# Moving query loads, masks and list products in an attention, dense and routed MLP kernel

## The chip, the cores and the metric

The kernel runs on one core of one Trainium2 chip. The metric is the device time of one execution in microseconds; the figure for a kernel is the median of its runs. A profile is taken of a separate execution, which has its own time and its own span (from the first to the last instruction).

## The reference

A delta-rule attention over 4 batches x 8 heads, 768 positions, 48 channels; then a dense gated MLP on the 3072 resulting tokens; then a routed MLP in which each token goes to one of 8 experts. Cut to what is computed:

```python
# attention, per batch and head
k_n = k / (norm(k) + 1e-6)
for t in range(768):
    y[t] = q[t] @ state
    v_old = k_n[t] @ state
    state += beta[t] * outer(k_n[t], v[t] - v_old)
# dense MLP ("MoE 1"), x is 3072 x 384
x = ((x @ w1) * (x @ w2)) @ w3 @ w_out
# routed MLP ("MoE 2")
logits = x @ w_gate + modality_bias[modality_id]
e_idx = argmax(logits); gate_w = softmax(logits)[e_idx]
out[mask_e] = gate_w * (relu(x[mask_e] @ w1[e]) @ w2[e])      # for each expert e
```

## The kernel before

**Stages.** `startup` (0 to about 120 us) decodes the dense weights, which arrive as raw 64-bit words, and folds `w3 @ w_out` into one matrix (product `pw`, 64 matmuls in 8 groups, the last operands of which, `wos`, lie partly in the buffer `X[1]`, called X_91 in the trace). Then `moe1(i)` runs 12 times, once for each tile of 256 tokens (about 41 us each). Each has 8 sub-steps `f`; a sub-step multiplies one slice of the first two weight matrices (`pAB`, 18 matmuls), evicts it (`a`, `ch`, `cl`), and two sub-steps later multiplies it by the folded matrix (`px`). At last `moe2` runs 14 slots of at most 256 tokens of one expert; a slot has 8 sub-steps of 9 matmuls `ph` and, two later, 6 matmuls `spy` (or `px` in every other slot).

**Attention steps.** The attention is cut into 12 steps `s` of 64 positions. Step `s` is done inside the tile `moe1(s - 1)`, by `slot(s, f)`. Its chain on TensorE: `chain_k` at f = 0 (keys times the state X, product `pk` or `pkq`), `chain_u` at f = 2 or 3 (`pu`), `chain_y` at f = 4 (`py`, the output), `chain_s` at f = 6 (`pS`, the next state). Every step also needs keys times queries with a causal mask, written over the queries, which lie beside the state in the same buffer (columns D and up of `X`, called W). From step 2 on state and queries are multiplied jointly: one matmul of 112 columns for the 48 of the state and the 64 of the queries (`pkq`). Steps 0 and 1 multiply the queries on their own (`masked`, product `pq`).

**PSUM rings.** Two pools of two buffers each, `ps` and `pc`. The joint product takes four buffers: quarters 0 and 1 from `ps`, 2 and 3 from `pc`. VectorE first subtracts the state's part of all four (R), then masks quarters 0 and 1 at f = 0; `mask_parts` yields, and quarters 2 and 3 are masked at f = 1. `chain_u`, `chain_y` and `chain_s` take buffers of `pc`; the products of `merge1`, `merge2`, `gram` and `place` take buffers of `ps`.

**Order.** Every engine's instructions are issued in the order in which the program is written (class `Engine` chains them), the DMA queue of SyncE (SP) too: an instruction that waits holds back all that stand behind it on its engine.

**Routed part.** `place` finds for each tile of tokens the place in the expert's list: a position (`pr`, then `pos`, `hi`, `lo` on VectorE), one-hot factors (`hot`), and their product `pl`, which is added to `list`. For the last tile this is done inside slot 0 of `moe2` by the generator `late`, of which `back` takes one piece in each sub-step; it goes on with the list (`listed`), and the table of the remaining slots (`late_slots`, `tif`), from which the token gathers of slot 3 and later start. `tokens2` transposes the gathered tokens of the next slot (`spt`, one product in each of three sub-steps) and splits them (`sxh` on ScalarE, `sxl` on VectorE); `weights` splits the next slot's weights (`w1h`, `w1l`, `w2h`, `w2l`). Two lines set their order in a sub-step:

```python
ahead(f in (1, 2, 3), 1 + (f < 3 if i == 0 else f > 4))   # back: tokens in which f, how many weight pieces
for _ in range(n): next(work, None)                        # step: weight pieces first, then tokens
```

Of the kernel before, what the change touches and what calls it, by code (L numbers as in the profile page):

```python
# [8 lines left out]
F32 = mybir.dt.float32  # L9
# [7 lines left out]
ALU = mybir.AluOpType  # L17
# [4 lines left out]
P = 128  # L22
B, H, S, D = 4, 8, 768, 48
NT, DM, DFF, E = 3072, 384, 1024, 8
NPAIR = H // 2
C = 64
# [79 lines left out]
class Kernel:  # L106
# [60 lines left out]
    def slot(self, s, f):  # L167

        if s >= NS:
            return  # L170
        u, c = divmod(s, US)
        self.at(s + f / FC)
        more = u + 1 < NUNIT
        if f == 0:
            self.chain_k(s)
            if s == 1:
                self.queries(1)
                self.queries(2)
        elif f == 1:
            if c == 0:  # L180
                list(self.merge1(u))
                next(self.work, None)
                if more:
                    self.work = self.inverse(u + 1)
            if s > 1:
                list(self.masks)
        elif f == 2:
            list(self.chain_u(s) if c else self.merge2(u))
            if s == 1:
                list(self.masked(s))  # L190
            if s + 1 < NS:
                self.values(s + 1)
        elif f == 3:
            if c == 0:
                list(self.chain_u(s))
            if c == 1 and u + 2 < NUNIT:
                self.keys(u + 2)
        elif f == 4:
            list(self.chain_y(s))
        elif f == 5:  # L200
            if s + 2 < NS:
                self.queries(s + 2)
            if c == 1 and u + 2 < NUNIT:
                self.prep(u + 2, range(0, NP, HP))
        elif f == 6:
            if s + 1 < NS:
                list(self.chain_s(s))
        elif f == 7:
            if s + 2 < NS:
                self.tokens(s + 2)  # L210
            if c == 1 and u + 2 < NUNIT:
                self.prep(u + 2, range(NP, NU, HP))
# [204 lines left out]
    def masked(self, s):  # L417

        nc, ps = self.nc, self.ps
        kT, W, n0 = self.st[s // US]["kT"], self.st["W", s], s % US * NP  # L420
        mb = self.mask.unsqueeze(1).to_broadcast([P, HP, C])
        todo = []
        for a in range(0, NP, HP):
            pq = ps.tile([P, HP, C], F32, tag="ps", name="pq")
            for n in range(HP):
                for h in range(2):
                    o, w = (1 - h) * C, h * C
                    nc.tensor.matmul(pq[o:o + C, n], kT[w:w + C, n0 + a + n], W[w:w + C, h, a + n], start=True, stop=True)
            todo.append((a, pq))
        yield  # L430
        for a, pq in todo:
            for h in range(2):
                o = (1 - h) * C
                if s < 1:
                    nc.scalar.copy(W[o:o + C, h, a:a + HP], pq[o:o + C])
                    nc.gpsimd.affine_select(out=W[o:o + C, h, a:a + HP], in_=W[o:o + C, h, a:a + HP], pattern=[[0, HP], [1, C]], compare_op=ALU.is_gt, fill=0.0, base=0, channel_multiplier=-1)
                    continue
                nc.vector.tensor_tensor(out=W[o:o + C, h, a:a + HP], in0=pq[o:o + C], in1=mb[o:o + C], op=ALU.mult)

    halves = range(0, NP, HP)  # L440

# [3 lines left out]
    def chain_k(self, s):  # L445

        nc, a1, pc = self.nc, self.a1, self.pc
        kT, n0, vt = self.st[s // US]["kT"], s % US * NP, self.st["v", s]
        self.scaled(s)
        if s == 0:  # L450
            self.R = vt
            return
        X = self.X[self.xi]
        R = a1.tile([P, NP, D], F32, tag="R", name="R")
        if s > 1:
            todo = []
            for q, a in enumerate(range(0, NP, NQ)):
                pool, tag = ((self.ps, "ps"), (pc, "pc"))[q // 2]
                pk = pool.tile([P, NQ, D + C], F32, tag=tag, name="pkq")
                for m in range(NQ):  # L460
                    for h in range(2):
                        o, w = (1 - h) * C, h * C
                        nc.tensor.matmul(pk[o:o + C, m], kT[w:w + C, n0 + a + m], X[w:w + C, h, a + m], start=True, stop=True)
                todo.append((a, pk))
            for a, pk in todo:
                nc.vector.tensor_tensor(out=R[:, a:a + NQ], in0=vt[:, a:a + NQ], in1=pk[:, :, 0:D], op=ALU.subtract)
            self.R = R
            self.masks = self.mask_parts(s, todo)
            next(self.masks)
            return  # L470
        for a in self.halves:
            pk = pc.tile([P, HP, D], F32, tag="pc", name="pk")
            for n, m, h in self.tiles(a):
                o, w = (1 - h) * C, h * C
                nc.tensor.matmul(pk[o:o + C, m], kT[w:w + C, n0 + n], X[w:w + C, h, n, 0:D], start=True, stop=True)
            nc.vector.tensor_tensor(out=R[:, a:a + HP], in0=vt[:, a:a + HP], in1=pk, op=ALU.subtract)
        self.R = R

    def mask_parts(self, s, todo):

        W = self.st["W", s]
        mb = self.mask.unsqueeze(1).to_broadcast([P, NQ, C])
        for q, (a, pk) in enumerate(todo):
            for h in range(2):
                o = (1 - h) * C
                self.nc.vector.tensor_tensor(out=W[o:o + C, h, a:a + NQ], in0=pk[o:o + C, :, D:], in1=mb[o:o + C], op=ALU.mult)
            if q == 1:
                yield
# [72 lines left out]
    def startup(self):  # L561
# [173 lines left out]
            do.setdefault(FC + 8 + x, []).append(lambda: next(rs, None))  # L735
        do.setdefault(t + 4, []).append(lambda: self.parts_x(0))
        folded = todo.index(("3", K3 - 1))
        do.setdefault(folded, []).append(self.clear)
        do.setdefault(folded + 1, []).append(lambda: split(self.chain_s(0)))
        do.setdefault(NSTART - 1, []).extend([lambda: self.tokens(1), lambda: self.tokens(2)])  # L740
        for n in range(-1, NSTART):
# [339 lines left out]
    def moe2(self, early, cur):  # L1081
# [3 lines left out]

        def late():
            yield
            yield from self.place(NT // MT - 1)
            yield
            yield from self.listed()  # L1090
            yield
            yield from self.late_slots()
# [22 lines left out]
        def ahead(i):  # L1115

            self.upto = i + 2
            toks = iter(self.tokens2(todo[i + 1], states[i + 1])) if i + 1 < len(kinds) else iter(())

            def step(tok, n):  # L1120
                for _ in range(n):
                    next(work, None)
                if tok:
                    next(toks, None)

            return step, toks
# [129 lines left out]
    def back(self, i, mi, ahead):  # L1256
# [11 lines left out]
        for f in range(FC):  # L1268
# [9 lines left out]
            hl = s3.tile([P, SLOT], F32R, tag="hl", name="hl", bufs=SLAG + 2)  # L1278
            nc.scalar.activation(hh, ph, AF.Relu)
            nc.vector.scalar_tensor_tensor(out=hl, in0=ph, scalar=0.0, in1=hh.bitcast(F32), op0=ALU.max, op1=ALU.subtract)  # L1280
            ahead(f in (1, 2, 3), 1 + (f < 3 if i == 0 else f > 4))
            if i < NEARLY:
                next(self.late, None)
            elif i > NEARLY + 1:
# [105 lines left out]
```

## Time and profile before

| | us |
|---|---|
| median of 3 runs | 841.74 (840.85 to 842.69) |
| the profiled execution, its own time | 841.03 |
| its span | 839.3 |
| TensorE busy in the span | 786.3 |
| VectorE busy | 618.8 |
| ScalarE busy | 408.9 |
| GpSimd busy | 165.6 |

The profiled execution's time is 1.7 us longer than its span, and 0.7 us below the median of the runs. Busy time is summed over instructions that overlap in part, so it tells which engine leads, not how much work is left. Each row of the timeline gives the start, the duration, the engine, and the tile written and the tiles read; in square brackets stands how long the engine sat idle before it and what ended that.

### The profile page before, as it was taken

The page shows a single profiled execution, that of the slowest core. Times are in us where ns is not written, and L with a number is a line of the kernel's source. Part 1 is how long each engine was busy: PE and PEld are TensorE (multiplying, and loading weights), DVE is VectorE, ACT ScalarE, POOL GpSimd, SP SyncE. Part 2 cuts the span into 40 slices and gives each one's busy share as a digit, 9 for nine tenths or more (in the row PEclk, how much of TensorE's full clock was granted, in tenths as well). Part 3 has the DMA queues.
Part 4 walks back from the last instruction along what each step waited for, and adds up shares of the span by engine and source line. Part 5 has one row for each costly group of instructions (what it writes and reads, how often), then busy time and mean ns, then how long its engine had stood idle before and what let it go on. Part 6 is the DMA issues. An engine that isn't in the chain of part 4 may idle for free.

```text
span 839.3 us, 23624 instructions
## 1 busy us (share of the span) xinstructions
PE 786.3 (94%) x9583; PEld 730.6 (87%) x9583; DVE 618.8 (74%) x1573; ACT 408.9 (49%) x863; POOL 165.6 (20%) x172
## 2 busy tenths in 40 slices
PE   5797789999999999999999999999899999999994
PEld 5664468999999899989998999999799999999983
DVE  5998889769777976897689864567886778677651
ACT  6467673562546154524543353334455655655541
POOL 3021121100000001000100000013254654645420
PEclk8598899999999999999999999999999999999997
DMA  9952563314121421133021401047457678677610
GB/s 310 280 176 87 151 161 102 75 35 120 54 51 38 116 65 40 40 115 82 23 65 39 102 13 31 27 131 222 151 177 246 215 249 258 227 225 238 220 56 6
DMA packets 71812, 105.34 MB, mean 126 GB/s; under 512 B 33988, under 2 KB 53332, under 8 KB 71696
## 3 DMA queue, kind: packets, MB, share of 16 engines
q1 hardware_dynamic: 64464, 88.35, 34.7%
q0 software_dynamic: 4064, 11.06, 3.9%
q10 hardware_dynamic: 3168, 4.34, 1.5%
q8 instruction: 77, 1.26, 0.6%
q14 instruction: 39, 0.32, 0.1%
HBM read 89.15 MB, written 10.63 MB: 119 GB/s over the span
## 4 chain that ended last, share of the span: by engine, by line
PE 46%; DVE 26%; issue 11%; ACT 7%; POOL 4%; DMA 3%; SPq 1%; POOLq 0%; DVEq 0%; ACTq 0%
PE pAB L86 13%; PE px L86 9%; PE ph L86 7%; PE spy L86 4%; DVE tmp L86 4%; DVE Tt L86 4%; DVE X L86 3%; DVE TT L86 2%; PE pw L86 2%; DVE Ab L86 2%; ACT TT L86 2%; PE pkq L86 2%; PE pg L86 2%; DVE a L86 2%; PE py L86 2%
## 5 line engine op out<-in xcount | busy, mean ns | idle before, releaser
L86 PE MATMUL pAB<-x,w 128*128 128x256 f32 x1728 | 228.8, 286 | 0.0
L86 PEld LDWEIGHTS pAB<-x,w 128*128 128x128 f32 x1728 | 213.9, 191 | 4.4
L86 ACT CAST ch<-a 128x256 fp32r<-128x256 f32 x96 | 39.0, 406 | 116.4 <-DVE a L86 116.4
L86 ACT COPY a<-pAB 128x256 f32<-128x256 f32 x96 | 35.6, 371 | 116.9 <-PE pAB L86 104.3
L86 DVE TENSOR_TENSOR a<-a,pAB 128x256 f32<-128x256 f32 x96 | 40.0, 416 | 65.6 <-ACT a L86 65.3
L86 PE MATMUL ph<-sxh,w1h 128*128 128x256 f32 x288 | 82.5, 286 | 0.5 <-DVE hl L86 0.5
L86 ACT ACTIVATE hh<-ph 128x256 fp32r<-128x256 f32 x96 | 37.0, 385 | 91.7 <-PE ph L86 91.5
L86 PE MATMUL ph<-sxl,w1h 128*128 128x256 f32 x288 | 81.2, 282 | 0.0
L86 PE MATMUL ph<-sxh,w1l 128*128 128x256 f32 x288 | 81.2, 282 | 0.0
L86 DVE SCALAR_TENSOR_TENSOR hl<-ph,hh 128x256 fp32r<-128x256 f32 x96 | 40.3, 420 | 41.0 <-ACT hh L86 40.5
L86 DVE TENSOR_TENSOR Tt<-tmp,Tt 128x31 f32<-128x31 f32 (+15 forms) x186 | 64.3, 346 | 6.4
L86 DVE TENSOR_TENSOR w2l<-r,w2h 128x768 fp32r<-128x768 f32 x56 | 59.5, 1074 | 12.2 <-ACT w2h L86 11.9
L86 DVE TENSOR_TENSOR tmp<-Ab,Tt 128x31 f32<-128x31 f32 (+15 forms) x186 | 65.4, 352 | 3.0
L86 PE MATMUL px<-w34h,ch 128*128 128x392 f32 x192 | 65.6, 342 | 0.0
L86 PE MATMUL px<-w34h,cl 128*128 128x392 f32 x192 | 65.3, 340 | 0.0
L86 PE MATMUL px<-w34l,ch 128*128 128x392 f32 x192 | 65.2, 339 | 0.0
L86 POOL TENSOR_TENSOR w1l<-r,w1h 128x512 fp32r<-128x512 f32 x39 | 51.0, 1327 | 49.9 <-ACT w1h L86 49.6
L86 DVE TENSOR_TENSOR cl<-a,ch 128x256 fp32r<-128x256 f32 x96 | 43.0, 447 | 20.1 <-ACT ch L86 19.3
L86 PEld LDWEIGHTS ph<-sxh,w1h 128*128 128x128 f32 x288 | 54.7, 190 | 1.3 <-DVE hl L86 1.1
L86 PEld LDWEIGHTS ph<-sxh,w1l 128*128 128x128 f32 x288 | 54.8, 190 | 0.0
L86 PEld LDWEIGHTS ph<-sxl,w1h 128*128 128x128 f32 x288 | 54.6, 190 | 0.0
L86 ACT CAST w1h<-r 128x512 fp32r<-128x512 f32 x84 | 49.5, 615 | 2.9 <-DMA r<-in_e_w_dram 2.5
(269 smaller groups left out, 1677.7 us busy)
## 6 DMA issues: line engine op xcount, KB each, us to landing
r<-in_e_w_dram SPq DMA_DIRECT2D x42, 512.0 KB, 4.7
r<-in_e_w_dram SPq DMA_DIRECT2D x56, 384.0 KB, 3.9
raw<-in_w_dram SPq DMA_DIRECT2D x28, 512.0 KB, 4.6
kT<-in_kt_dram SPq DMA_DIRECT2D x12, 512.0 KB, 4.5
X<-in_q_dram SPq DMA_DIRECT2D x24, 256.0 KB, 4.8
vt<-in_v_dram SPq DMA_DIRECT2D x12, 384.0 KB, 4.7
kb<-in_kb_dram SPq DMA_DIRECT2D x12, 384.0 KB, 4.7
x2d<-xr ACTq DMA_DIRECT2D x22, 192.5 KB, 2.8
```

The source lines that it names most:

```text
L86: x = f(*a, **kw)
```

## The change

It does five things.

1. Step 1 multiplies state and queries jointly as well (`chain_k`); its mask is applied by a ScalarE copy and a GpSimd select (`mask_parts`) in place of VectorE's products, in eight pieces of 64 x 256. `masked` is left with step 0 alone.
2. The query loads of steps 1 and 2 are issued in `startup`, when the last fold has been issued, in place of sub-step 0 of tile 0.
3. The joint product's rings change places with the step's parity: odd steps take quarters 0 and 1 from `pc`, 2 and 3 from `ps`.
4. In slot 0 of the routed part the product `pl` and its addition to `list` come one sub-step later; in slot 0 the next slot's token piece comes ahead of the weight pieces of the sub-step.
5. In slot 2 the transposes for slot 3 come in sub-steps 3, 4, 5 in place of 1, 2, 3.

```diff
@@ slot @@
         if f == 0:
             self.chain_k(s)
-            if s == 1:
-                self.queries(1)
-                self.queries(2)
...
-            if s > 1:
-                list(self.masks)
+            list(self.masks)
         elif f == 2:
             list(self.chain_u(s) if c else self.merge2(u))
-            if s == 1:
-                list(self.masked(s))
@@ chain_k @@
+        for q, a in enumerate(range(0, NP, NQ)):
+            pool, tag = ((self.ps, "ps"), (pc, "pc"))[(q // 2 + s) % 2]
-                pool, tag = ((self.ps, "ps"), (pc, "pc"))[q // 2]
...
-        for a in self.halves:
-            pk = pc.tile([P, HP, D], F32, tag="pc", name="pk")
...
@@ mask_parts @@
+                if s == 1:
+                    self.nc.scalar.copy(W[o:o + C, h, a:a + NQ], pk[o:o + C, :, D:])
+                    self.nc.gpsimd.affine_select(out=W[o:o + C, h, a:a + NQ], in_=W[o:o + C, h, a:a + NQ], pattern=[[0, NQ], [1, C]], compare_op=ALU.is_gt, fill=0.0, base=0, channel_multiplier=-1)
+                    continue
@@ startup @@
-        do.setdefault(folded, []).append(self.clear)
+        do.setdefault(folded, []).extend([self.clear, lambda: self.queries(1), lambda: self.queries(2)])
@@ moe2, late @@
-            yield from self.place(NT // MT - 1)
+            last = self.place(NT // MT - 1)
+            next(last)
             yield
+            next(last)
+            yield
+            yield
+            list(last)
             yield from self.listed()
@@ moe2, step @@
+                if tok and i == 0:
+                    next(toks, None)
                 for _ in range(n):
                     next(work, None)
-                if tok:
+                if tok and i > 0:
                     next(toks, None)
@@ back @@
-            ahead(f in (1, 2, 3), 1 + (f < 3 if i == 0 else f > 4))
+            ahead(f - 2 * (i == 2) in (1, 2, 3), 1 + (f < 3 if i == 0 else f > 4))
```

The DMA queue of SP at the end of `startup`; `raw` are pieces of the dense weights, X_91 and X_90 the buffers of the queries of steps 1 and 2, `kb` the keys by token of steps 1 and 2. Before:

```order
L86 DMA raw<-in_w_dram 128x512 x13
L86 DMA kb<-in_kb_dram 128x768 x2
L86 DMA X_91<-in_q_dram 64x16x64 x2
L86 DMA X_90<-in_q_dram 64x16x64 x2
L86 DMA vt<-in_v_dram 128x768
```

and now:

```order
L86 DMA raw<-in_w_dram 128x512 x12
L86 DMA X_91<-in_q_dram 64x16x64 x2
L86 DMA X_90<-in_q_dram 64x16x64 x2
L86 DMA raw<-in_w_dram 128x512
L86 DMA kb<-in_kb_dram 128x768 x2
```

The four query loads went ahead of the last weight piece and of the two `kb` loads.

TensorE at sub-step 3 of slot 0 of the routed part, where the list's product `pl` reads `hot`; the `spy` behind it is of sub-step 1. Before:

```order
L86 MATMUL ph<-sxh,w1l 128x256
L86 MATMUL spt<-ident,xg 128x128 x2
L86 LDWEIGHTS hot
L86 MATMUL pl<-hot 128x192
L86 LDWEIGHTS hot
L86 MATMUL pl<-hot 128x192
L86 MATMUL spy<-w2h,hh 128x384
```

and now, with the `ph` of sub-step 4 ahead of it and the `spy` of sub-step 2 behind:

```order
L86 MATMUL ph<-sxh,w1l 128x256
L86 LDWEIGHTS hot
L86 MATMUL pl<-hot 128x192
L86 LDWEIGHTS hot
L86 MATMUL pl<-hot 128x192
L86 MATMUL spy<-w2h,hh 128x384
```

The list's product stands 15 matmuls later (6 `spy` and 9 `ph`).

VectorE at sub-step 1 of the same slot, where `sxl` frees the buffer that the second transpose waits for, and `pos` begins the last tile's placing. Before:

```order
L86 SCALAR_TENSOR_TENSOR hl<-ph,hh 128x256
L86 TENSOR_TENSOR w1l<-r,w1h 128x512
L86 TENSOR_TENSOR sxl<-spt,sxh 128x256
L86 TENSOR_TENSOR pos<-pr,cnt 128x16
L86 TENSOR_TENSOR cnt<-pr,cnt 128x8
```

and now:

```order
L86 SCALAR_TENSOR_TENSOR hl<-ph,hh 128x256
L86 TENSOR_TENSOR sxl<-spt,sxh 128x256
L86 TENSOR_TENSOR w1l<-r,w1h 128x512
L86 TENSOR_TENSOR pos<-pr,cnt 128x16
L86 TENSOR_TENSOR cnt<-pr,cnt 128x8
```

The token split and one weight piece changed places.

## Rows read from the trace of the kernel before

**Rows 1.** The page: busy us of each engine, share of the span, instructions.
```profile
PE 786.3 (94%) x9583; PEld 730.6 (87%) x9583; DVE 618.8 (74%) x1573; ACT 408.9 (49%) x863; POOL 165.6 (20%) x172
```

**Rows 2.** TensorE's waits over the whole span: us in total, times, longest us.
```profile
PE pu L86 <- DVE X L86: 4.1, 4, 1.4
...
PE py L86 <- DVE X L86: 1.6, 3, 1.0
...
PE pkq L86 <- DVE list L86: 1.0, 2, 0.6
```

**Rows 3.** Timeline, TensorE, step 5 (start us, us, engine, instruction, idle before).
```profile
283.03 2.52 PE L86 MATMUL pkq<-X,kT 64*64 64x112 f32 x48 [0.61 <-DVE list L86]
...
293.09 2.07 PE L86 MATMUL pu<-R,TT 64*64 64x48 f32 x64 [0.87 <-DVE X L86]
```

**Rows 4.** Timeline, VectorE, step 5: the two mask parts of the joint product.
```profile
288.10 1.73 DVE L86 TENSOR_TENSOR X<-pkq,mask 64x256 f32<-64x256 f32 x4
...
292.09 1.75 DVE L86 TENSOR_TENSOR X<-pkq,mask 64x256 f32<-64x256 f32 x4
```

**Rows 5.** Timeline, TensorE: step 1's two products, and step 3's joint one.
```profile
118.81 2.12 PE L86 MATMUL pk<-X,kT 64*64 64x48 f32 x64 [0.41 <-ACT X L86]
...
127.31 1.97 PE L86 MATMUL pq<-X,kT 64*64 64x64 f32 x60
...
200.02 3.37 PE L86 MATMUL pkq<-X,kT 64*64 64x112 f32 x64
```

**Rows 6.** Timeline, VectorE: step 1's masks.
```profile
136.06 2.85 DVE L86 TENSOR_TENSOR X<-pq,mask 64x512 f32<-64x512 f32 x4
```

**Rows 7.** Timeline, GpSimd and SP: what waits for the last fold, the last weight piece.
```profile
114.98 2.80 POOL L86 MEMSET X<- 32x1536 f32 x2 [19.40 <-PE pw L86]
...
116.38 0.33 SPq L86 DMA_DIRECT2D raw<-in_w_dram  x1
```

**Rows 8.** Landing of query loads: the four of steps 1 and 2.
```profile
DMA to landing us min/median/max: 5.7/7.7/8.0
```

**Rows 9.** The same for one later step's pair, and SP's issue of it.
```profile
190.45 1.30 SPq L86 DMA_DIRECT2D X<-in_q_dram  x2
...
DMA to landing us min/median/max: 4.0/4.3/4.6
```

**Rows 10.** Timeline, GpSimd and VectorE: step 0's selects, VectorE under them and alone.
```profile
53.88 3.33 POOL L86 TENSOR_SCALAR_AFFINE_SELECT X<-X 64x512 f32<-64x512 f32 x4 [45.24 <-ACT X L86]
...
53.98 0.67 DVE L86 TENSOR_TENSOR tmp<-Ab,Tt 128x112 f32<-128x112 f32 x1
...
82.40 0.27 DVE L86 TENSOR_TENSOR tmp<-Ab,Tt 128x112 f32<-128x112 f32 x1
```

**Rows 11.** Stretches: length, then PE, PEld, DVE, ACT, POOL busy (count), PEclk, DMA.
```profile
95.70:102.50 6.80, 3.41 (x5) 1.85 (x6) 6.56 (x13) 3.87 (x9) 0.00 (x0) 0.50 0.49 163
...
597.50:600.80 3.30, 3.30 (x15) 3.30 (x14) 1.39 (x3) 0.00 (x0) 0.00 (x0) 0.50 0.52 204
```

**Rows 12.** Timeline, TensorE, slot 0: the waits, and the spy of sub-step 2.
```profile
592.13 0.44 PE L86 MATMUL spt<-ident,xg 128*128 128x128 f32 x2 [1.15 <-DVE sxl L86]
...
596.75 0.64 PE L86 MATMUL pl<-hot 128*128 128x192 f16 x2 [1.84 <-DVE hot L86]
...
600.90 0.34 PE L86 MATMUL spy<-w2h,hh 128*128 128x384 f32 x1
```

**Rows 13.** Timeline, VectorE, slot 0: token split, and the hl of sub-steps 2 and 3.
```profile
591.66 0.42 DVE L86 TENSOR_TENSOR sxl<-spt,sxh 128x256 fp32r<-128x256 f32 x1
...
595.54 0.42 DVE L86 SCALAR_TENSOR_TENSOR hl<-ph,hh 128x256 fp32r<-128x256 f32 x1
...
597.00 0.42 DVE L86 SCALAR_TENSOR_TENSOR hl<-ph,hh 128x256 fp32r<-128x256 f32 x1
```

**Rows 14.** Timeline, TensorE, slot 2: its first product, and the wait for gathered tokens.
```profile
628.04 0.28 PE L86 MATMUL ph<-sxh,w1h 128*128 128x256 f32 x1
...
632.04 0.33 PE L86 MATMUL spt<-ident,xg 128*128 128x128 f32 x1 [1.59 <-DMA xg<-x2d,id]
```

More of the change, by code (lines that the diff above doesn't have):

```diff
@@ L420, in masked @@
         kT, W, n0 = self.st[s // US]["kT"], self.st["W", s], s % US * NP
-        mb = self.mask.unsqueeze(1).to_broadcast([P, HP, C])
         todo = []
@@ L433, in masked @@
                 o = (1 - h) * C
[L434 to L438, printed above, removed]
+                nc.scalar.copy(W[o:o + C, h, a:a + HP], pq[o:o + C])
+                nc.gpsimd.affine_select(out=W[o:o + C, h, a:a + HP], in_=W[o:o + C, h, a:a + HP], pattern=[[0, HP], [1, C]], compare_op=ALU.is_gt, fill=0.0, base=0, channel_multiplier=-1)
     halves = range(0, NP, HP)
@@ L454, in chain_k @@
         R = a1.tile([P, NP, D], F32, tag="R", name="R")
-        if s > 1:
-            todo = []
-            for q, a in enumerate(range(0, NP, NQ)):
-                pool, tag = ((self.ps, "ps"), (pc, "pc"))[q // 2]
[L459 to L470, printed above, removed]
-        for a in self.halves:
-            pk = pc.tile([P, HP, D], F32, tag="pc", name="pk")
[L473 to L476, printed above, removed]
+        todo = []
+        for q, a in enumerate(range(0, NP, NQ)):
+            pool, tag = ((self.ps, "ps"), (pc, "pc"))[(q // 2 + s) % 2]
+            pk = pool.tile([P, NQ, D + C], F32, tag=tag, name="pkq")
+            for m in range(NQ):
+                for h in range(2):
+                    o, w = (1 - h) * C, h * C
+                    nc.tensor.matmul(pk[o:o + C, m], kT[w:w + C, n0 + a + m], X[w:w + C, h, a + m], start=True, stop=True)
+            todo.append((a, pk))
+        for a, pk in todo:
+            nc.vector.tensor_tensor(out=R[:, a:a + NQ], in0=vt[:, a:a + NQ], in1=pk[:, :, 0:D], op=ALU.subtract)
         self.R = R
+        self.masks = self.mask_parts(s, todo)
+        next(self.masks)
     def mask_parts(self, s, todo):
```

## The prediction

> **What bounds the kernel now.** I read the page first: TensorE is busy in 94% of the span, the next engine, VectorE, in 74% [rows 1]. So the time is TensorE's own work plus its waits, and an edit is worth what it takes from either. The table of TensorE's waits then shows which waits the change can touch [rows 2], and the timeline of one place each shows what the wait hangs on: in the odd attention steps [rows 3, 4], in step 1 [rows 5 to 9], in slot 0 of the routed part [rows 12, 13], and in slot 2 [rows 14]. The reader is to see in the rows that these waits are short (0.4 to 1.8 us) and that each ends with a VectorE instruction or a transfer that stands late in its order, not with one that lacks time. Last comes the granted clock by stretches: there are stretches in which TensorE ran at 1.2 GHz, the lower level, and one of them follows on the waits of slot 0 [rows 11].
>
> **Rings by parity (odd steps).** In step 5 `pu` waits 0.87 us for a mask [rows 3]: `chain_u` takes its two buffers from `pc`, and there quarters 2 and 3 of the joint product lie, which are masked last, from 292.09 on; quarters 0 and 1 are done at 288.10 + 1.73 = 289.83 [rows 4]. Now quarters 0 and 1 lie in `pc`. `pu` would be reached at 293.09 - 0.87 - 0.61 = 291.6 (the 0.61 is the wait of the next sentence), 1.8 us after its buffers are free. That 1.8 us is the cover: if VectorE ran later by more than that, the rest would come back as a wait. There are four such waits, 4.1 us in all [rows 2]. The joint product itself waits in two odd steps for the `list` addition, which frees a `ps` buffer, 1.0 us in all [rows 2, 3]; it now begins in `pc`, and comes to `ps` half a product (1.7 us of the 3.37 in rows 5) later, over the longest of these waits, 0.6. Nothing is late next: the second mask part is then needed only by `py`, two sub-steps on, and the even steps keep their rings. Sum: -5.1, bounds 0 and -5.1; I take -5.1, because the rows name the masks and the list as what ended these waits.
>
> **Step 1, joint.** Removed: the state's product, 2.12, and the queries' own, 64/60 of 1.97 = 2.10; added: a joint one, 3.37 in step 3 [rows 5]. That is -0.85 on TensorE. VectorE loses four masks, 2.85 us [rows 6], behind which `py` waited three times, 1.6 us in all [rows 2]; that wait goes, since the masks now go to ScalarE and GpSimd sub-steps before `py`. Together -2.45.
>
> Against it stands that the joint product needs the queries at once. Their loads write into X_91, where the last fold still reads. The GpSimd clearing of the same buffer begins at 114.98, released by that fold [rows 7], and the loads can't be issued before it either. A pair takes 1.30 us to issue [rows 9], so the second goes out at about 115.65. To its landing the rows give two prices: 4.0 to 4.6 us for a pair with nothing ahead of it [rows 9], and 5.7 to 8.0 for these very loads, which before had a weight piece and two `kb` loads ahead of them [rows 7, 8]. The bounds are thus 115.65 + 4.0 = 119.7 and 115.65 + 8.0 = 123.6. I take 4.6, so 120.3, because of the three loads ahead only one weight piece is left, issued earlier. TensorE was to begin at 118.81 [rows 5], so it waits 1.5 us longer. Sum of step 1: -2.45 + 1.5 = -0.9. The bounds: -2.45 if no wait is added, +2.4 at 123.6.
>
> A rule bears on that choice. The Trainium skill, DMA: Bandwidth & Descriptors, section Queues, rings and completion order, says that a DMA engine takes up descriptors of one queue in the order of its ring. By it the two loads for step 2 and the weight piece behind them can't hold up those of step 1, and the sum would be the -0.9; with the longest landing seen here it would be +2.4. The rows of before do not separate the two, since there the heavier loads were ahead as well as beside.
>
> The eight GpSimd selects are half the size of step 0's, four of which took 3.33 us [rows 10]: 8 x 0.42 = 3.3 us on an engine that is busy for a fifth of the span. VectorE isn't free of them: a product over 112 columns took 0.67 us under those selects and 0.27 without [rows 10]. Four products so stretched by 0.4 us are 1.6 us, less than the 2.85 us of masks that VectorE loses. The Trainium skill, SBUF — State Buffer, section Who interferes with whom, has a harder rule: a VectorE instruction with two inputs in SBUF and a GpSimd one that reads SBUF block each other for the whole instruction. By it VectorE could lose all 3.3 us, 0.5 more than it gains, and the wait of `py` would come back with about 0.5 us of its 1.6; the trace shows the stretching, and does not show whether it is whole.
>
> ScalarE gets eight copies of 64 x 256. VectorE's masks of that shape take 1.73 / 4 = 0.43 [rows 4]; at that price it is 3.5 us on an engine that is busy for half of the span, spread over two sub-steps, and I cost it at nothing. If that cover were gone, `a` of the same sub-step would be late by it, and `pAB` two sub-steps on behind that. On SP the four loads now stand ahead of the last weight piece (116.38 before, rows 7) and of two `kb` loads. Four at 0.65 us each from 115.0 put the piece at 117.6 or later; it is decoded in tile 0 and `kb` is first needed at sub-step 6, so I cost this at nothing too, and return to it below.
>
> **Slot 0 of the routed part.** The second transpose waited 1.15 us for `sxl`, which ended at 592.08; it now stands ahead of one weight split, whose place began 0.6 us earlier [rows 12, 13]: -0.6. The list's product waited 1.84 us up to 596.75, so TensorE was there at 594.91 [rows 12], now at 594.3. It goes on with six `spy` (0.175 us each, 1.05), to 595.35. The `ph` of sub-step 4 then needs the buffer that `hl` of sub-step 2 frees at 595.54 + 0.42 = 595.96 [rows 13]: a new wait of 0.6. Nine `ph` at 0.117 take it to 597.05, where `hot` is ready (`hl` begins behind it at 597.00, rows 13); the product takes 0.2, and the `spy` of sub-step 2 begins at 597.3 in place of 600.90 [rows 12]: -3.6. Of that 1.65 is the low clock: the stretch from 597.50 to 600.80 ran at 1.2 GHz [rows 11], half speed for 3.3 us. I take it that the clock stays up, because the waits of this place (1.15 and 1.84 among them) shrink to about 1.2 us. If it falls all the same, the sum is -1.95. The addition to `list` comes a sub-step later than before, but `listed` still follows in the same sub-step as before, so the chain to the table is not lengthened.
>
> **Slot 2.** The transposes waited 1.59 us for gathered tokens, to 632.04 [rows 14]. Slot 2 would begin at 628.04 - 3.6 = 624.4. The new place is four `ph` groups and one `spy` group in, 5.3 us, so 629.7. The table on which the gathers hang is made by VectorE in pieces behind the `hl` of each sub-step, so it moves up with TensorE by some part of 3.6: tokens between 628.4 and 632.0, a wait between 0 and 2.3. I take 0, as the pieces follow TensorE's sub-steps: -1.6; the other end is +0.7.
>
> **Sum.** -5.1 - 0.9 - 3.6 - 1.6 = -11.2. The profiled execution took 841.03, so 829.8; the median of the runs was 0.7 above it (841.74), so 830.5.
>
> **Rivals.**
> - *The stall of step 1 pulls the clock down.* TensorE is idle for about 1.9 us before the joint product (from 118.4, its wait of before included), more than either wait in slot 0 that was followed by 1.2 GHz. For it: the stretch from 95.7 to 102.5, in which TensorE was busy for only half, ran at 1.2 GHz throughout [rows 11]. Against it: the wait of 1.59 in slot 2 stands alone and is no longer than that by much, and no fall of the clock is among its rows. One such stretch costs 1.65: 832.2. With the late landing (+3.3) and 6.8 us at half speed (3.4): 837.2.
> - *The gain of the routed part is eaten.* The clock falls in slot 0 anyway (+1.65), and the tokens of slot 3 do not move up (+2.3): 834.4. For it: VectorE is the engine that ends every wait there. Against it: the two long waits shrink by more than half.
> - *The rings don't do it.* The `pu` waits stay because VectorE is late in general, and only the list waits go: +4.1, so 834.6. Against it: the first masks are done 1.8 us before `pu` is reached.
> - *Slower.* The query loads, four with 64-column pieces, and the weight piece behind them hold TensorE up at step 1. Each microsecond of landing past 120.3 costs one, and the low clock 3.4 more. That eats the whole gain at 120.3 + 11.2 - 3.4 = 128.1, 12.5 us after issue; at 16 us after issue (131.6) the kernel would take 841.7 + 3.5 = 845.2. The longest landing in the rows is 8.0 [rows 8], so this needs a queue twice as slow as any seen.
>
> **How the numbers follow.** Chances: the forecast 0.44, the stall with the clock 0.29, the routed part 0.11, the rings 0.06, slower 0.05, and 0.05 for several losses together that end near the time before. Likeliest: 830.5. The range goes from 828.8 (no wait for the queries, -1.5 more) to 837.2, and leaves out the last two cases and the tails. A measurement of this kernel tells some 0.2% (1.7 us) from no change; so faster 0.90, same 0.05, slower 0.05.
>
> **What would show it.** Right: no waits of `pu` for masks and of `pkq` for `list` in steps 3 to 9; the joint product of step 1 at about 120.3; no wait of `py` in step 1; full clock in slot 0 and the `spy` of its sub-step 2 about 3.6 us earlier against the slot's start; no wait for `xg` in slot 2. Wrong: a joint product of step 1 after 122 or with PEclk 0.5 behind it, new waits of `pAB` for `a` in tile 0 or for `hl` in slots 0 and 1, or tokens of slot 3 that come no earlier than before.

## Result and the profile after

The changed kernel takes 832.33 us (median of 4 runs, 829.90 to 832.64), the kernel before 842.22 (4 runs). The ratio is 0.9878, with a 95% interval of 0.9855 to 0.9901: faster by 1.2%, some 10 us. The forecast was 830.5 in a range of 828.8 to 837.2, so the time lies 1.8 us above the forecast and inside the range. Measured again for the experiments (e5 below), the same kernel took 832.03 against 840.36, a ratio of 0.9895 (0.9877 to 0.9914).

The profiled execution took 832.64 us, with a span of 830.4. From the page, as in [rows 1]:

```profile
PE 782.0 (94%) x9519; PEld 727.6 (88%) x9519; DVE 617.9 (74%) x1571; ACT 410.9 (49%) x871; POOL 170.0 (20%) x180
```

TensorE is busy 4.3 us less and the span is 8.9 us shorter; the rest, about half, is time in which TensorE waited. The table of TensorE's waits (us in total, times, longest), to be read against [rows 2]; rows of the startup, which differ by up to 1.2 us either way, are left out, as are waits that stayed as they were:

```profile
PE ph L86 <- DVE hl L86: 1.5, 2, 1.1
...
PE pkq L86 <- ACT X L86: 1.4, 1, 1.4
...
PE pkq L86 <- DMA X<-in_q_dram: 1.0, 1, 1.0
PE pkq L86 <- ACT An L86: 0.7, 2, 0.4
...
PE spt L86 <- DVE sxl L86: 0.5, 1, 0.5
...
PE spy L86 <- DVE hl L86: 0.2, 1, 0.2
```

The waits of `pu` and `py` for masks, of `pkq` for `list`, of `pl` and of `spt` for `xg` are gone. New are the two waits of step 1's joint product (1.4 and 1.0), a longer one for `hl` in slot 0, and one of `spy`; the wait of `pkq` for `An` grew from 0.2 to 0.7.

To see where the time went, the span is cut at six starts that can be read from TensorE's timeline: the first `pS`, the `pAB` of sub-step 4 of tile 0, and the first `ph` of slots 0 to 3. Each column is a difference of two such starts (us), for every kernel profiled here:

| kernel | to first pS | step 1 | rest of MoE 1 | slot 0 | slot 1 | slot 2 | slot 3 to end |
|---|---|---|---|---|---|---|---|
| before | 116.76 | 23.28 | 446.58 | 23.71 | 17.71 | 19.43 | 191.83 |
| after | 116.26 | 24.44 | 440.72 | 20.60 | 17.71 | 18.56 | 192.11 |
| e1 rings off | 117.07 | 27.14 | 446.40 | 20.60 | 17.71 | 18.94 | 191.84 |
| e2 rings only | 116.94 | 23.24 | 440.84 | 22.16 | 17.71 | 19.17 | 191.84 |
| e3 step 1 old | 117.34 | 23.25 | 440.78 | 20.63 | 17.71 | 18.92 | 193.07 |
| e4 fill | 116.20 | 21.21 | 440.84 | 20.60 | 17.74 | 19.20 | 191.71 |
| e5 after again | 116.54 | 22.41 | 440.76 | 20.62 | 17.71 | 19.81 | 192.65 |
| e6 before again | 116.26 | 23.26 | 446.16 | 23.71 | 17.72 | 19.52 | 191.77 |
| e7 pl back | 117.76 | 22.55 | 440.93 | 24.04 | 17.74 | 18.72 | 191.76 |
| e8 tokens back | 116.27 | 22.56 | 440.96 | 20.21 | 17.72 | 19.24 | 191.74 |
| e9 slot 2 back | 117.66 | 22.35 | 440.86 | 20.62 | 17.72 | 19.49 | 191.90 |
| e10 fewer pieces | 116.88 | 22.32 | 440.77 | 20.61 | 17.73 | 17.77 | 196.02 |
| e11 three edits | 115.57 | 21.24 | 441.07 | 20.23 | 17.71 | 17.74 | 197.84 |
| e12 step 2 later | 115.58 | 22.41 | 440.70 | 20.61 | 17.74 | 18.44 | 191.92 |

Where nothing was edited, "rest of MoE 1" and slots 0 and 1 repeat within 0.4 us. The other columns do not: without an edit in them the startup differs by up to 2.2 us between executions, slot 2 and the last column by 1.4 each. So effects below 2 us are read from the columns and not from the total times, and in slot 2 not from one profile.

Step 1 in the changed kernel, on TensorE (start, us, engine, instruction, idle before and what ended it), and PEclk behind it in the view by stretches (columns as in [rows 11]):

```profile
116.26 1.64 PE L86 MATMUL pS<-X,kb 64*48 64x48 f32 x64
119.33 0.37 PE L86 MATMUL pkq<-X,kT 64*64 64x112 f32 x2 [1.43 <-ACT X L86]
120.69 4.91 PE L86 MATMUL pkq<-X,kT 64*64 64x112 f32 x62 [0.98 <-DMA X<-in_q_dram]
...
130.04 2.07 PE L86 MATMUL pu<-R,TT 64*64 64x48 f32 x64
...
138.68 2.08 PE L86 MATMUL py<-X 128*64 128x64 f32 x64
...
122.00:125.40 3.40, 3.40 (x40) 3.32 (x35) 1.87 (x5) 2.44 (x6) 1.38 (x4) 0.50 1.00 328
```

The joint product stalls twice, for 2.41 us together, and then 62 of its matmuls take 4.91 us, because the clock fell to 1.2 GHz. `pu` and `py` wait for nothing any more.

Slot 0, TensorE, as in [rows 12]: the second transpose, the `ph` of sub-step 4, the list's product:

```profile
586.32 0.44 PE L86 MATMUL spt<-ident,xg 128*128 128x128 f32 x2 [0.54 <-DVE sxl L86]
...
591.21 0.39 PE L86 MATMUL ph<-sxh,w1h 128*128 128x256 f32 x1 [1.07 <-DVE hl L86]
...
592.37 0.34 PE L86 MATMUL pl<-hot 128*128 128x192 f16 x2
```

`pl` no longer waits, `spt` waits 0.61 less than before, and the wait for `hl` that the forecast put at 0.6 is 1.07.

The end of slot 2, which has a wait that was not there before. From the timelines of GpSimd, VectorE, SP, ScalarE and TensorE, in the order in which one waits for the other:

```profile
628.68 2.55 POOL L86 TENSOR_TENSOR w1l<-r,w1h 128x512 fp32r<-128x512 f32 x2
...
628.87 3.19 DVE L86 TENSOR_TENSOR w2l<-r,w2h 128x768 fp32r<-128x768 f32 x1 [0.29 <-ACT w2h L86]
...
632.08 0.35 SPq L86 DMA_DIRECT2D r<-in_e_w_dram  x1
...
635.75 0.62 ACT L86 CAST w1h<-r 128x512 fp32r<-128x512 f32 x1 [2.25 <-DMA r<-in_e_w_dram]
636.28 0.38 ACT L86 ACTIVATE hh<-ph 128x256 fp32r<-128x256 f32 x1
...
637.49 0.45 PE L86 MATMUL spy<-w2h,hl 128*128 128x384 f32 x1 [0.16 <-DVE hl L86]
```

VectorE's `w2l` split takes 3.19 us beside two GpSimd splits (0.94 for the last one of this slot, at 635.04, with GpSimd idle). It ends at 632.06, SP issues the next weight load at 632.08, the ScalarE cast that needs a load starts at 635.75, and the `hh` of sub-step 7 is queued behind that cast. That the load issued at 632.08 is the one waited for is inferred from the order; the landings of single loads aren't in these rows. The other profiles bear it out. In the eight whose slot 2 is that of the changed kernel (after, e1, e3, e4, e5, e7, e8, e12) the cast waits 2.11 to 3.48 us for the load and begins 3.57 to 4.03 us after the end of `w2l`, and slot 2 takes 16.31 to 16.34 us more than this wait in every one of them. So the whole spread of slot 2, 18.44 to 19.81 us, is this one wait. In e5 it is longest:

```profile
635.30 0.62 ACT L86 CAST w1h<-r 128x512 fp32r<-128x512 f32 x1 [3.48 <-DMA r<-in_e_w_dram]
```

### The profile page after: what moved, and what is told of

The parts are those of the page before. It is cut to its first block, busy times and chain, and to the rows that moved or that the text cites. A ratio compares the mean times of both kernels' runs of the same rounds, so it can differ in the third digit from the quotient of the medians.

```text
span 830.4 us, 23512 instructions
## 1 busy us (share of the span) xinstructions
PE 782.0 (94%) x9519; PEld 727.6 (88%) x9519; DVE 617.9 (74%) x1571; ACT 410.9 (49%) x871; POOL 170.0 (20%) x180
## 4 chain that ended last, share of the span: by engine, by line
PE 71%; DVE 10%; issue 9%; POOL 4%; DMA 3%; ACT 2%; SPq 0%; POOLq 0%; DVEq 0%; ACTq 0%
PE pAB L86 26%; PE px L86 16%; PE ph L86 8%; PE pkq L86 4%; PE spy L86 3%; DVE TT L86 3%; PE py L86 3%; PE pu L86 3%; PE pS L86 2%; PE pg L86 2%; POOL w1l L86 2%; DVE tmp L86 2%; PE pe L86 1%; PE pf L86 1%; POOL out_dram L86 1%
```

## Experiments

The kernel before was measured anew beside the experiments: the times of e1 to e4 stand against 840.21 us for it, those of e5 to e8 against 840.36, those of e9 to e12 against 840.41.

**e1, the ring exchange undone in the changed kernel.**

```diff
-            pool, tag = ((self.ps, "ps"), (pc, "pc"))[(q // 2 + s) % 2]
+            pool, tag = ((self.ps, "ps"), (pc, "pc"))[q // 2]
```

> The changed kernel with one part undone: the joint product takes quarters 0 and 1 from ps in every step. Theory (the ring is what pu and pkq waited for): the four waits of pu for masks (about 4.1 us) and the two of pkq for the list addition (1.0 us) come back, and the stretch from the pAB of sub-step 4 of tile 0 to slot 0 grows from 440.7 us by at least 5.1; the kernel takes about 837.5 us. Rival (VectorE is late in general, the ring does not matter): no such waits, the stretch stays at about 441 and the time at 832.3.

Measured: 840.43 us, ratio 1.000 (0.998 to 1.002). All of the gain is gone. "Rest of MoE 1" is 446.40 again, as expected, and step 1 takes 27.14 us, which was not. TensorE in step 1, and the clock under the joint product:

```profile
121.35 3.25 PE L86 MATMUL pkq<-X,kT 64*64 64x112 f32 x62 [0.95 <-ACT TT L86]
...
132.07 2.42 PE L86 MATMUL pu<-R,TT 64*64 64x48 f32 x64 [2.98 <-ACT X L86]
...
121.35:124.60 3.25, 3.25 (x63) 3.10 (x63) 2.73 (x6) 2.12 (x5) 0.00 (x0) 1.00 1.10 263
```

With the old rings, quarters 2 and 3 of step 1 lie in `pc`, and `pu` waits 2.98 us for the ScalarE copies that free them. So the exchange is also what makes step 1's new form pay: it is worth 5.7 us in the later steps and 4.7 (27.14 - 22.41) in step 1. The last row was a surprise too: after waits of 1.31 and 0.95 us the clock stayed up.

**e2, the ring exchange alone**, the same line edited in the kernel before.

> The kernel before with the ring exchange of odd steps alone. Theory: the waits of pu (4.1 us) and of pkq for list (1.0 us) go and nothing takes their place, so 842.2 - 5.1 = 837.1 us. The same stretch became 5.9 shorter under the whole change; if the 0.8 us beyond the waits belongs to the rings as well, 836.3. Rival (it needs step 1 in the joint form too, or other parts): gain below 2 us, 840 or more.

Measured: 834.71 us, ratio 0.9939 (0.9923 to 0.9955), a gain of 5.1 us (3.8 to 6.5). "Rest of MoE 1" falls by 5.74 (by 5.32 against the second profile of the kernel before, e6); the two kinds of wait summed to 5.1 (4.8 in e6), so some 0.5 to 0.6 belongs to six restarts of TensorE or to what else isn't resolved. Unexpected was slot 0, which e2 doesn't edit: 22.16 us against 23.71. The waits there are the same to the hundredth, but the clock didn't fall behind them:

```profile
591.15 0.64 PE L86 MATMUL pl<-hot 128*128 128x192 f16 x2 [1.84 <-DVE hot L86]
...
592.50:595.80 3.30, 3.30 (x27) 3.30 (x26) 1.92 (x5) 1.11 (x2) 0.00 (x0) 1.00 0.46 174
```

In the 3.30 us from 592.50 TensorE ran 27 matmuls; in the same stretch of the kernel before 15, at PEclk 0.50 [rows 11].

**e3, step 1 as before in the changed kernel**: the state's product and `masked` apart, VectorE's masks, the query loads in sub-step 0 of tile 0.

```diff
-        do.setdefault(folded, []).extend([self.clear, lambda: self.queries(1), lambda: self.queries(2)])
+        do.setdefault(folded, []).append(self.clear)
@@ slot @@
+            if s == 1:
+                self.queries(1)
+                self.queries(2)
...
+            if s == 1:
+                list(self.masked(s))
...
```

> The changed kernel with step 1 as before: queries multiplied on their own, VectorE's masks, query loads in sub-step 0 of tile 0. Theory (step 1 in the joint form lost 1.2 us, because the stall pulled the clock down): the stretch from the first pS to the pAB of sub-step 4 of tile 0 goes back from 24.4 to 23.3 us, the clock stays up after 122 us, and the kernel takes about 831.2. Rival (the term of the forecast, a gain of 0.9): 833.2.

Measured: 832.95 us, ratio 0.9905 (0.9878 to 0.9933), step 1 23.25 us. The theory, made from one profile of the changed kernel, fell: that profile's 24.44 is the exception. In the seven other profiles in which the joint product waits like this (e1, e5, e7 to e10, e12) the clock stayed up under it, and in the six of them with the new rings step 1 took 22.3 to 22.6. So the joint form gains 0.7 to 0.9 us, as forecast.

**e4, TensorE's wait filled**: step 1's joint product behind the `pAB` of sub-step 0 of tile 0.

```diff
         if f == 0:
-            self.chain_k(s)
+            if s != 1:
+                self.chain_k(s)
@@ moe1, behind the 18 matmuls of pAB @@
+            if i + LEAD == 1 and f == 0:
+                self.chain_k(1)
```

> The changed kernel with one move: step 1's joint product stands behind the pAB of sub-step 0 of tile 0 in place of ahead of it, so that TensorE has 2.3 us of work while the queries land. Theory (the stall is what brought the 1.2 GHz stretch): a wait of at most 0.5 us for the queries, the joint product at full clock in 3.4 us, and the stretch from the first pS to the pAB of sub-step 4 goes from 24.4 to about 20.7; 828.6 us. Rival (the clock falls for another reason: the joint product itself, or what precedes the stall): only the 2.0 us of waiting go, the joint product still takes 5 us with PEclk 0.5; 830.2. Second rival: VectorE or ScalarE is now late with R or a, and a wait of pu or pAB takes the gain; 832 or more.

Measured: 829.95 us, ratio 0.9874 (0.9847 to 0.9902). TensorE:

```profile
117.77 2.41 PE L86 MATMUL pAB<-x,w 128*128 128x256 f32 x18
120.11 3.76 PE L86 MATMUL pkq<-X,kT 64*64 64x112 f32 x64
...
137.41 2.41 PE L86 MATMUL pAB<-x,w 128*128 128x256 f32 x18 [0.53 <-DVE a L86]
```

The queries cost no wait that the profile names (3.76 against 3.37 in [rows 5] for the same 64 matmuls), and 0.53 us come back as a wait for `a`. Step 1 takes 21.21 us, 1.2 less than the changed kernel at full clock and 3.2 less than in its first profile. By its median it is the fastest of all kernels here that were run more than once. Whether it keeps the clock from falling can't be told, since the clock stayed up in most profiles without it.

**e5 and e6, both kernels once more, unaltered**, because of what e1 and e2 showed of the clock.

> The changed kernel once more, nothing altered, for a second profile. Theory A (a stall at this place always brings the 1.2 GHz stretch): the waits of step 1's joint product are again about 2.4 us, PEclk is again 0.5 from 122 to 125 us, and the stretch from the first pS to the pAB of sub-step 4 of tile 0 is again 24.4 us. Theory B (whether the clock falls behind a wait differs from one execution to the next, as the ring experiments suggest, where longer waits kept PEclk at 1.00): the same waits, but perhaps full clock and then about 22.8.

> The kernel before once more, nothing altered. Theory A: behind the waits of slot 0 (1.15 and 1.84 us) the clock falls again and slot 0 takes 23.7 us. Theory B (by execution): the same waits; slot 0 takes 22.2 us if the clock stays up, as it did with the rings alone.

Measured: the changed kernel 832.03 us; the kernel before 840.23 (one run). The joint product in e5, then the `pl` of slot 0 and the clock behind it in e6:

```profile
120.60 3.25 PE L86 MATMUL pkq<-X,kT 64*64 64x112 f32 x62 [0.96 <-DMA X<-in_q_dram]
...
120.60:123.90 3.30, 3.30 (x63) 3.15 (x64) 2.58 (x6) 2.20 (x5) 0.00 (x0) 1.00 1.10 263
```

```profile
595.81 0.64 PE L86 MATMUL pl<-hot 128*128 128x192 f16 x2 [1.84 <-DVE hot L86]
...
596.60:599.90 3.30, 3.30 (x16) 3.30 (x15) 1.35 (x3) 0.00 (x0) 0.00 (x0) 0.54 0.67 204
```

In e5 the waits of the joint product are 1.09 and 0.96, and the clock stays up: theory B for step 1. In e6 the clock falls again in slot 0, with the waits at which it stayed up in e2. So at neither place do the waits alone decide. For step 1 one and the same kernel shows both levels; in slot 0 the profile without the fall is of another kernel (e2), so what decides there stays open. The two waits of step 1 summed to 2.41 us in the one profile in which the clock fell and to 1.96 to 2.26 in the seven in which it didn't; whether that small difference counts stays open.

**e7, the list's product one sub-step earlier again**, and **e8, tokens behind the weight pieces again**, each in the changed kernel.

```diff
-            last = self.place(NT // MT - 1)
-            next(last)
+            yield from self.place(NT // MT - 1)
             yield
-            next(last)
-            yield
-            yield
-            list(last)
             yield from self.listed()
```

```diff
-                if tok and i == 0:
-                    next(toks, None)
                 for _ in range(n):
                     next(work, None)
-                if tok and i > 0:
+                if tok:
                     next(toks, None)
```

> The changed kernel with the list's product one sub-step earlier, as before; tokens still ahead of the weight pieces in slot 0. Theory (the later product is what took the long wait): pl waits again, some 1.8 us less what the tokens gained, hl no longer 1.07; slot 0 takes 21.6 us at full clock (23.2 with a 1.2 GHz stretch) against 20.6; 833.3. Rival (VectorE is full in slot 0, so any order costs the same): 20.6 and 832.3.

> The changed kernel with the tokens of slot 0 behind the weight pieces, as before; the list's product still late. Theory of the forecast: the second transpose waits 1.15 us again in place of 0.54, so slot 0 takes 21.2 us against 20.6. Rival (VectorE is full up to sub-step 4, and the wait for hl there takes up what the earlier wait leaves): the wait for hl shrinks from 1.07 to about 0.5 and slot 0 stays at 20.6.

Measured: e7 833.86 us, ratio 0.9911 (0.9887 to 0.9936), slot 0 24.04; e8 830.85 (one run), slot 0 20.21. The `pl` of e7 and the clock behind it, then the second transpose and the `pl` of e8:

```profile
591.75 0.72 PE L86 MATMUL pl<-hot 128*128 128x192 f16 x2 [2.85 <-DVE hot L86]
...
592.00:594.00 2.00, 1.86 (x8) 1.92 (x8) 1.89 (x5) 0.00 (x0) 0.00 (x0) 0.51 0.53 209
```

```profile
585.30 0.44 PE L86 MATMUL spt<-ident,xg 128*128 128x128 f32 x2 [1.15 <-DVE sxl L86]
...
590.36 0.34 PE L86 MATMUL pl<-hot 128*128 128x192 f16 x2
```

In e7 TensorE reaches `pl` earlier and waits 2.85 us, because VectorE isn't done sooner: the later product is what brought slot 0's gain. The clock fell there too, and 24.04 is 0.8 above the 23.2 that was expected with such a fall. Of the 3.4 us between 24.04 and 20.6 the fall makes some 1.55 (what it cost in slot 0 of the kernel before: 23.71 - 22.16), an estimate, and the order the rest. In e8 the transpose waits 0.61 longer and the wait for `hl` of 1.07 is gone altogether, so the order of before is better by 0.4 us beside the late product. Neither side had expected that. VectorE has little room here: from the start of slot 0 to `pl` it is busy for 9.96 of 10.95 us in the changed kernel and for 9.58 of 10.57 in e8.

**e9, slot 2's transposes in their old place**, and **e10, two weight pieces fewer late in slot 2**.

```diff
-            ahead(f - 2 * (i == 2) in (1, 2, 3), 1 + (f < 3 if i == 0 else f > 4))
+            ahead(f in (1, 2, 3), 1 + (f < 3 if i == 0 else f > 4))
```

```diff
-            ahead(f - 2 * (i == 2) in (1, 2, 3), 1 + (f < 3 if i == 0 else f > 4))
+            ahead(f - 2 * (i == 2) in (1, 2, 3), 1 + (f < 3 if i == 0 else f == 5 if i == 2 else f > 4))
```

> The changed kernel with the transposes of slot 2 back in sub-steps 1, 2, 3. The gathers moved up by 3.1 us with slot 0 and land about 1.4 us before the transposes of the changed kernel read them. Theory of the forecast: in the old place they are again waited for, by 1.9 us, so slot 2 takes about 19.7 us; the changed kernel's own slot 2 was 18.6 to 19.8. Rival (the move only trades the wait for xg against the one for hh and hl at the slot's end): the end of slot 2 is free of waits again and slot 2 takes 19.1 to 19.4, as the mean of the changed one.

> The changed kernel with two weight pieces fewer in sub-steps 6 and 7 of slot 2 (all later pieces come two places later). Theory (at the end of slot 2 ScalarE stands at a w1h of slot 4 whose load has not landed, and the hh of sub-step 7 is queued behind it): the piece now stands behind that hh, no wait of spy, slot 2 takes 17.9 us in place of 18.6 to 19.8, and later slots stay as they are. Rival (VectorE's w2l, stretched to 3 or 4 us beside GpSimd, is what makes hl late): the wait stays, 18.6 to 19.8.

Measured: e9 832.71 us (one run), slot 2 19.49, with this wait:

```profile
623.25 0.33 PE L86 MATMUL spt<-ident,xg 128*128 128x128 f32 x1 [1.63 <-DMA xg<-x2d,id]
```

The wait for gathered tokens is back with 1.63 us in place of 1.59 before [rows 14]. The end of slot 2 is free of waits, as the rival had it. Slot 2 with the moved transposes took 18.44 to 19.81 in the eight profiles named above (mean 18.98). So against this one profile the move gains 0.5 on the mean, and in a single execution anything from a gain of 1.05 to a loss of 0.3: the rival was nearer.

e10: 834.20 us (one run). Slot 2 took 17.77, as the theory had it, and without a wait, though `w2l` still took 3.18 us. So the piece at the end of slot 2 is what held `hh` up. But slots 3 and later took 4.2 us more, which the theory denied. TensorE, VectorE and GpSimd there:

```profile
652.66 0.44 PE L86 MATMUL px<-w2h,hl 128*128 128x384 f32 x1 [0.66 <-DVE hl L86]
...
680.13 0.39 PE L86 MATMUL ph<-sxh,w1h 128*128 128x256 f32 x1 [1.56 <-DVE hl L86]
...
676.56 3.18 DVE L86 SCALAR_TENSOR_TENSOR fh<-nf,first 1x9 f32<-1x9 f32 x1
...
677.20 2.51 POOL L86 TENSOR_TENSOR w1l<-r,w1h 128x512 fp32r<-128x512 f32 x2
```

All later pieces moved by two places, and GpSimd's splits met other VectorE instructions: one of nine elements, which took 0.15 us in every profile with the old places, took 3.18 us beside two of them. Four new waits of TensorE for `hl`, 3.1 us together, make up most of the 4.2.

**e11, three edits together**: those of e4, e8 and e10.

> The changed kernel with three edits: step 1's joint product behind the pAB of sub-step 0, tokens behind the weight pieces in slot 0 as before, and two weight pieces fewer in sub-steps 6 and 7 of slot 2. By the stretches: step 1 21.2 us (22.4 to 24.4 in the changed kernel), slot 0 20.2 (20.6), slot 2 17.9 if the theory of the weight pieces holds, else about 19.1. Against the changed kernel -2.2 to -3.2 and -0.4 and -1.2 or 0: 828 to 829.5 us.

Measured: 832.30 us, ratio 0.9912 (0.9895 to 0.9929), above the 828 to 829.5 expected. Step 1 (21.24), slot 0 (20.23) and slot 2 (17.74) came out as in e4, e8 and e10, and the loss behind slot 2 (197.84 against about 191.8) takes all of it back. The edits of e4 and e8 alone, which should come to about 829.5, were not run.

**e12, the query loads of step 2 in sub-step 0 of tile 0 again**, those of step 1 at the last fold.

```diff
-        do.setdefault(folded, []).extend([self.clear, lambda: self.queries(1), lambda: self.queries(2)])
+        do.setdefault(folded, []).extend([self.clear, lambda: self.queries(1)])
@@ slot @@
             self.chain_k(s)
+            if s == 1:
+                self.queries(2)
```

> The changed kernel with the query loads of step 2 issued in sub-step 0 of tile 0 again; those of step 1 stay at the last fold. Theory (loads of one queue are served in the order of issue, so those behind cost nothing): the second load of step 1 lands where it did, 6.2 us after the pair's issue began, and the joint product begins 4.4 us after the first pS. Rival (loads in flight share the engines): it lands up to 1.3 us earlier, since only two query loads are in flight, and the joint product begins 3.1 us after the first pS.

Measured: 829.48 us (one run), step 1 22.41. TensorE's joint product, and SP's issue of the last weight piece:

```profile
119.66 3.25 PE L86 MATMUL pkq<-X,kT 64*64 64x112 f32 x62 [0.92 <-DMA X<-in_q_dram]
...
115.18 1.51 SPq L86 DMA_DIRECT2D raw<-in_w_dram  x1
```

The first `pS` was at 115.58, so the second query load let TensorE go on 4.08 us later; in e5, with all four loads together, 4.06 (120.60 - 116.54), and in the seven profiles with four together in which the joint product waits, 3.98 to 4.43. Taking the loads of step 2 away from behind changed nothing, as the theory had it. But the edit did not leave the loads of step 1 alone in flight, as the rival supposed: the weight piece and the two `kb` loads moved up behind them (the piece was issued at 115.18, in e5 only at 118.91). So e12 shows that it made no difference which of these loads stood behind; whether loads behind cost anything at all stays open.

## Why the prediction was right, step by step

- **Rings, -5.1.** Right in mechanism, too small: -5.3 to -5.7 (446.16 and 446.58 to 440.84 in e2). The bound of -5.1 was the sum of the waits' rows. What the forecast did not see is that step 1's new form rests on the exchange (e1).
- **Step 1, -0.9.** 23.28 to 22.41 is -0.87. The terms were off, and made up for each other: TensorE went on 2.0 us later after `pS` than before (4.06 against 118.81 - 116.76 = 2.05), not 1.5: the second load came later than the 4.6 us after its issue that the forecast took (5.6 us in the first profile). The work fell by 0.71 and not 0.85 (from 5.89 to 5.18 us for joint product or `pk`, `pu` and `pq`). The stretch from `pAB` of sub-step 2 to that of sub-step 4, which holds `py`, fell by 2.17 (10.83 to 8.66) where the waits in it were 1.6: as with the rings, more went than the idle time of the waits. The three sum to -0.87. VectorE under the selects lost far less than either price in the forecast: its products there took up to 0.51 us in place of 0.42.
- **The queue rule** of the Trainium skill (DMA: Bandwidth & Descriptors, Queues, rings and completion order) is in agreement with e12, where a change of the loads issued behind didn't delay those ahead, 4.08 against 4.06 us. No run here leaves them without any load behind, so it is not shown that such loads cost nothing.
- **Slot 0, -3.6.** Measured -3.11. The work term of -1.95 was mis-sized: at full clock on both sides it is 22.16 (e2) to 20.60, -1.56, mainly because the new wait for `hl` was 1.07 and not 0.6. The forecast's 0.6 for the tokens was a gain at one place only: e8 shows that the token order, with the late product, costs 0.4. The clock's 1.65 measured 1.55 (23.71 against 22.16): it stood in both profiles of the kernel before and was absent in e2 beside the same waits, so the waits alone don't set it, though the forecast had them do so.
- **Slot 2, -1.6.** This is the step that failed: -0.4 on the mean (19.37 over before, e2 and e6; 18.98 with the change). That the gathers follow slot 0 was right: a wait of 0. The forecast did not name what is late next. TensorE's work moved up against GpSimd's, `w2l` met the GpSimd splits, and a weight load, a ScalarE cast and `hh` followed: the cast's wait of 2.11 to 3.48 us sets the length of slot 2 to within 0.03 us, and with the cast out of the way (e10) slot 2 is -1.6, the forecast's term.
- **Sum.** The four terms as measured are -8.1 to -8.6 at full clock, and -9.7 to -10.1 where the clock fell in slot 0 of the kernel before only. The measured medians differ by 9.9 and 8.3, the forecast had 11.2. Slot 2 fell short by 1.2 and slot 0 by 0.5, and the rings gave 0.2 to 0.6 more than forecast: that the time came within 1.8 us of the forecast is in part luck.
- **Rivals.** The stall that pulls the clock down (832.2) is what the first profile of the changed kernel shows, to the term: a fall of 1.66 (4.91 for 62 matmuls against 3.25 in e5). The median agrees with that number by chance; e5 has the same time without it, and loses in slot 2 and after. The others did not come: no load landed near the 12.5 us after issue from which the kernel would have been slower.

## What to carry to other kernels

When a wait is removed, follow the next engine in the same sub-step until something has slack: here the moved transposes met a cast, a weight load and GpSimd's splits, and kept a quarter of their gain. A change that frees a buffer ring may carry another change of the same diff, so undo parts one by one and add up stretches, not totals. Where single executions differ, look across all profiles at hand for the wait that goes with the difference, as the cast's wait does with slot 2. A term that hangs on the clock belongs into the range and not into the sum, unless several profiles of the same kernel show it.

## What the runs showed of the hardware

- **VectorE beside GpSimd.** A VectorE instruction on nine elements took 3.18 us (e10) where GpSimd ran two splits of 2.51 us together, and 0.15 elsewhere. The `w2l` split took 3.19 us beside two of them in the changed kernel, against 0.94 alone. In e5 it was longer still:

```profile
627.20 4.07 DVE L86 TENSOR_TENSOR w2l<-r,w2h 128x768 fp32r<-128x768 f32 x1 [0.30 <-ACT w2h L86]
...
627.90 2.55 POOL L86 TENSOR_TENSOR w1l<-r,w1h 128x512 fp32r<-128x512 f32 x2
...
636.26 0.44 PE L86 MATMUL spy<-w2h,hh 128*128 128x384 f32 x1 [0.83 <-ACT hh L86]
```

  `w2l` started 0.70 us ahead of the splits and ended 0.82 after them: 0.70 + 2.55 + 0.82 is the 4.07. The same end holds everywhere: of the 122 `w2l` splits in all profiles here that overlap with GpSimd splits, 121 end 0.81 to 0.83 us after the last of these, whether they started after the first or up to 0.70 us ahead of it. The other one started 0.80 us ahead and took 0.96. So the early start gained `w2l` nothing, and VectorE stayed out through two GpSimd instructions in a row. The Trainium skill (SBUF — State Buffer, Who interferes with whom) says that a VectorE instruction with two inputs in SBUF contends with a GpSimd one that reads SBUF, and that this is an exclusive lock. The trace agrees for the splits. For the selects of step 1 both engines lost a little, in e5 up to 0.51 against 0.42 us for a product and 0.48 to 0.67 against 0.41 for a select:

```profile
131.00 2.44 POOL L86 TENSOR_SCALAR_AFFINE_SELECT X<-X 64x256 f32<-64x256 f32 x4 [5.05 <-ACT X L86]
...
131.43 0.51 DVE L86 TENSOR_TENSOR tmp<-Ab,Tt 128x256 f32<-128x256 f32 x1
```

- **The clock.** The same waits of TensorE (0.46, 1.15 and 1.84 us in slot 0) were followed by 1.2 GHz in the two profiles of the kernel before and by 2.4 GHz in that of e2. Where the clock fell, TensorE ran 15 matmuls in 3.3 us in place of 27, and slot 0 took 1.55 us longer.
